# Squared-ReLU attention and a gated feed-forward: the first quad's k and q loaded by SyncE and cast on chip, with a new order of the work

## The chip, the cores and the metric

The kernel runs on one core of a Trainium2 chip. The metric is the device time of one execution in microseconds: the median of the runs, and lower is better. The profile comes from one further execution, taken by the hardware profiler; its times are counted from the first instruction of the program (the span's start).

A core has TensorE (PE, with its weight loads as PEld), VectorE (DVE), ScalarE (ACT), GpSimd (POOL) and SyncE (SP, which here only issues DMAs). Each engine works through its own queue in order. DMAs issued by SP and by POOL are carried out by the same 16 DMA engines.

## What is computed

```python
def _attn_ref(q, k, v):                       # q, k, v: (8, 12, 448, 64) float32
    scale = 1.0 / np.sqrt(q.shape[-1])
    scores = scale * np.matmul(q, k.transpose(0, 1, 3, 2))
    attn = np.maximum(scores, 0.0) ** 2 / S   # S = 448
    return np.matmul(attn, v)

def _moe_ref(x, w_in, w_out):                 # x: (3584, 768), w_in: (768, 2048)
    h = x @ w_in
    g = h * (1.0 / (1.0 + np.exp(-1.702 * h)))
    return g @ w_out                          # out: (3584, 768) float32
```

The attention's output, heads side by side, is the `x` of the feed-forward part.

## The kernel before

**Tiling.** The 96 heads are worked in 24 units of four heads, called quads (u = 0 to 23, three to a batch element). A quad's 448 positions are split into J = 7 blocks of 64. The feed-forward part works on eight groups of tokens, g = 0 to 7, alternately of 6 and 8 blocks (384 and 512 columns, `gblk`). Group 0 needs quads 0, 1 and 2.

**How k and q come in.** There are two ways, and both end in transposed float16 tiles `kT` and `qT`.

- Quads 0 to 5: `load16` (L115) lets POOL issue a DMA that casts float32 to float16 on the way, 448 KB read and 224 KB written. `trans_pe` (L124) then transposes on PE with 14 small matmuls (L129) into a PSUM bank of the pool `ps_m`, which has two, and VectorE copies the result out (L133).
- Quads 6 to 23: `load_qk` (L77) lets SP issue two plain DMAs of float32 (L82) into the tiles `kst` and `qst`, two buffers each. `cast` (L96) turns k into float16 on ScalarE (L102) and q on POOL (L104), and `trans` (L107) transposes by DMA (L111).

The float16 tiles `k16` and `q16` have three buffers each. v always comes by POOL's casting DMA (L91), and so do the weights, `win` in four quarters (L383, two DMAs each) and `wout` in four (L388, indexed by half of the columns and half of the rows).

**What is done with them.** A slot `s u.j` (L138, L145) makes the scores of block j in one of three PSUM pairs (`ps_s`): four matmuls, two by two, on quarters of the array. `relu2` (L152) takes the positive part, on ScalarE (L159) or, where the token has `:d`, on VectorE (L156); `:h` holds it back until after the next feed-forward product, and `:t` issues the slot's matmuls twice. The square `x u.j` is a VectorE product (L430). `a u` multiplies by v (28 matmuls, L174) and `xt_evac` (L182) copies the result into the group's `xt` (L194, L197). `f g.c` (L214) makes one of 16 chunks of the hidden layer, six matmuls (L222), the activation on ScalarE (L227) and a scaling on POOL (L229). Groups 1 to 7 multiply two blocks of rows at a time by `wout` in seven products `p g.m.n` (L303) instead of eight, which needs sums of the halves of `wout`. VectorE makes these sums in the tokens A to E (L272). Group 0 uses plain products `m g.m.h` (L242).

**What sets the order.** Nothing is scheduled by the compiler: the kernel holds a list of 729 words (L459 to L508) which is run from left to right, and each word issues its instructions on each engine's queue in that order. So the list is the order of every queue. Before it stand a warm-up of ScalarE's table and ten matmuls on a zero tile (L405). The list begins:

```python
"jq0 jk0 I q0 k0 z3 s0.0:d x0.0 s0.1 x0.1 jq1 jk1 s0.2 q1 s0.3 x0.2 x0.3 s0.4 k1 "
"x0.4 z3 jk4 jk2 s0.5 s0.6 k2 k4 x0.5 s1.0 s1.1 jv0 x0.6 s1.2 jq3 x1.0 x1.1 a0:m "
```

`jq`, `jk`, `jv` are POOL's casting loads of q, k and v; `jw` and `jo` load parts of `win` and `wout`. `q` and `k` are the transposes on PE, `z3` is three more zero matmuls into a fresh score bank, and `I` makes the identity for the transposes (on POOL). `L`, `K`, `Q`, `R` are load, two casts and transposes of the second way, `W` a later load of v. `G1` is a DMA of 128 bytes that holds SP's queue until a part of `wout` has landed, and stands ahead of the first `L` (SP has nothing to do before it).

Of the kernel before, what the change touches and what calls it, by code (L numbers as in the profile page):

```python
# [8 lines left out]
F32 = mybir.dt.float32  # L9
# [6 lines left out]
def kernel(  # L16
# [9 lines left out]
    nc = tc.nc  # L26
# [88 lines left out]
    def load16(u, n):  # L115
# [5 lines left out]
            in_=quad({"k": k, "q": q}[n], b, pr))  # L121
        st[n + "16"] = x

    def trans_pe(u, n):  # L124
        st = units[u]
        ps = ps_m.tile([128, 1024], F16, name="tr", tag="mm")
        for j in range(J):
            for a in range(2):
                nc.tensor.matmul(  # L129
                    out=ps[64 * a:64 * a + 64, j * 128:(j + 1) * 128],  # L130
                    lhsT=st[n + "16"][:, a, j, :], rhs=ident[:, :], is_transpose=True)
        t = qkT.tile([128, J, 128], F16, name=f"{n}T", tag=f"{n}T")
        nc.vector.tensor_copy(out=t, in_=ps[:, 0:J * 128])  # L133
        st[n + "T"] = t

    early = []

    def scores(u, j, times=1):  # L138
        st = units[u]
        sc = early.pop() if early else ps_s.tile([128, 2, 512], F32, name="sc", tag="sc")  # L140
        for s in [0, 1] * times:
            for a in range(2):
                r = slice(64 * a, 64 * a + 64)
                c = slice(64 * s, 64 * s + 64)
                nc.tensor.matmul(  # L145
                    out=sc[c, a, 0:S],
                    lhsT=st["kT"][r, j, c],
                    rhs=st["qT"][r, :, c],
                    start=True, stop=True)
        return sc  # L150

    def relu2(u, j, sc, dve=False):  # L152
        rl = rlp.tile([128, 2, S], F16, name="rl", tag="rl")
        at = atp.tile([128, 2, S], F16, name="at", tag="at")
        if dve:
            nc.vector.tensor_scalar(out=rl, in0=sc[:, :, 0:S], scalar1=0.0, scalar2=None,  # L156
                                    op0=ALU.max)
        else:
            nc.scalar.activation(out=rl, in_=sc[:, :, 0:S], func=AF.Relu)  # L159
        pend[u, j] = (at, rl)  # L160
        return at

# [232 lines left out]


    with tc.manual_schedule():
        nc.vector.memset(warm, 0.0)
        nc.scalar.activation(out=warm, in_=warm, func=AF.Gelu_apprx_sigmoid)

# [18 lines left out]
                   "D": (w_d, wout[1][0], wout[0][0], ALU.add)}  # L419

        def slot(how, u, j):
            sc = scores(u, j, 2 if "t" in how else 1)
            if "h" in how:
                held.append((u, j, sc))
            else:
                ats[u, j] = relu2(u, j, sc, "d" in how)
# [13 lines left out]
        def zeros(how, n):  # L440
            early.append(ps_s.tile([128, 2, 512], F32, name="sc", tag="sc"))
            for _ in range(n):
# [6 lines left out]
              "f": lambda how, g, f: m1(g, f), "m": lambda how, g, m, h: m2(g, m, h),  # L449
              "p": lambda how, g, m, n: pair(g, m, n), "i": lambda how, g, m, h: single(g, m, h),  # L450
              "jk": lambda how, u: load16(u, "k"), "jq": lambda how, u: load16(u, "q"),
              "jv": lambda how, u: load_v(u), "jw": lambda how, i: w1(i),
              "jo": lambda how, h, i: w2(h, i), "I": lambda how: make_identity(nc, ident),
              "G": lambda how, i: sp_gate(wout[0][i][0:1, 0, 0:64]),
# [2 lines left out]
              "Q": lambda how, u: cast(u, "q", nc.gpsimd),  # L457
              "R": lambda how, u: trans(u)}
        words = (  # L459
            "jq0 jk0 I q0 k0 z3 s0.0:d x0.0 s0.1 x0.1 jq1 jk1 s0.2 q1 s0.3 x0.2 x0.3 s0.4 k1 "  # L460
            "x0.4 z3 jk4 jk2 s0.5 s0.6 k2 k4 x0.5 s1.0 s1.1 jv0 x0.6 s1.2 jq3 x1.0 x1.1 a0:m "
            "s1.3 s1.4 x1.2 jq2 s1.5 jk3 q2 jk5 x1.3 x1.4 jv2 s1.6 x1.5 jv1 k3 s2.0:t q3 x1.6 "
            "jw0 s2.1:t x2.1 s2.2:t x2.0 s2.3:t x2.2 a1:m x2.3 s2.4:t jq4 jq5 s2.5:t s2.6 x2.4 "
            "x2.5 x2.6 jv3 jw1 jv4 k5 s3.0 jv5 a2 s3.1 q4 jw2 x3.0 x3.1 s3.2 f0.0 q5 x3.2 jw3 "
            "s3.3:d s3.4 x3.3 s3.5 x3.4 jo0.1 f0.1 f0.2 s3.6 s4.0:d x3.5 s4.1 f0.3 f0.4 x4.0 G1 "
            "x3.6 a3 x4.1 s4.2 x4.2 jo0.0 s4.3 x4.3 f0.5 L6 f0.6 s4.4 s4.5:h x4.4 s4.6:d f0.7 "
            "f0.8 L7 f0.9 x4.6 f0.10 x4.5 s5.0:d x5.0 s5.1 a4 s5.2 s5.3 f0.11 x5.2 f0.12 jo1.1 "
            "x5.1 x5.3 s5.4 s5.5:d x5.4 s5.6 f0.13 f0.14 x5.5 f0.15 K6 Q6 x5.6 R6 a5 m0.2.0 "
            "f1.0 C0 m0.1.0 f1.1 K7 m0.0.0 s6.0:d s6.1 Q7 L8 s6.2 x6.0 A3 f1.2 f1.3 f1.4 f1.5 "
            "x6.2 s6.3 s6.4:h x6.1 E0 Q8 s6.5:d x6.3 x6.5 W6 R7 jo1.0 f1.6 A1 f1.7 s6.6 C3 s7.0 "  # L470
            "f1.8 x6.6 x6.4 K8 x7.0 f1.9 f1.10 L9 s7.1 Q9 R8 a6 L10 W7 s7.2 s7.3 E3 A2 f1.11 "
            "x7.1 C1 x7.2 K9 R9 x7.3 f1.12 s7.4:h s7.5 x7.5 m0.0.1 B3 B0 s7.6 B1 x7.6 x7.4 K10 "
            "Q10 s8.0 s8.1 x8.0 x8.1 f1.13 m0.1.1 A0 s8.2 x8.2 W8 a7 s8.3:d s8.4 L11 B2 m0.2.1 "
            "s8.5 x8.4 x8.3 s8.6 f1.14 D3 x8.5 x8.6 f1.15 W9 s9.0:d s9.1 x9.0 a8 R10 L12 s9.2 "
            "s9.3 p1.0.0 K11 f2.0 f2.1 C2 f2.2 x9.2 f2.3 x9.1 s9.4 s9.5:h x9.3 s9.6 p1.0.1 f2.4 "
            "D1 f2.5 f2.6 x9.4 E2 f2.7 s10.0 Q11 L13 x9.6 K12 s10.1:h s10.2:h x9.5 x10.0 f2.8 "
            "p1.0.2 x10.1 p1.0.3 Q12 x10.2 s10.3 a9 E1 x10.3 s10.4:d s10.5 f2.9 W10 f2.10 f2.11 "
            "R11 f2.12 p1.0.4 R12 x10.4 x10.5 s10.6 x10.6 s11.0 D0 s11.1 D2 f2.13 x11.0 W11 "
            "x11.1 p1.0.5 s11.2 a10 L14 s11.3:h s11.4 p1.0.6 x11.4 x11.2 Q13 K13 p1.2.0 f2.14 "
            "s11.5 x11.3 s11.6 f2.15 x11.5 p1.2.1 x11.6 L15 p1.2.2 s12.0 a11 s12.1 x12.0 "  # L480
            "s12.2:h p1.2.3 Q14 p1.2.4 s12.3 R13 x12.1 K15 s12.4:h K14 s12.5 x12.2 p1.2.5 "
            "p1.2.6 f3.0 f3.1 x12.5 x12.4 x12.3 s12.6:h s13.0:h s13.1 Q15 i2.2.1 R14 x13.1 "
            "i2.2.0 x13.0 L16 W12 p2.0.0 p2.0.1 s13.2:h L17 x12.6 a12 s13.3 f3.2 R15 f3.3 W13 "
            "x13.2 x13.3 f3.4 f3.5 p2.0.2 f3.6 s13.4 Q16 s13.5 s13.6 x13.4 f3.7 x13.5 W14 x13.6 "
            "f3.8 s14.0:d Q17 s14.1 x14.1 s14.2:h x14.0 K16 f3.9 W15 L18 p2.0.3 f3.10 x14.2 a13 "
            "s14.3 s14.4 f3.11 f3.12 x14.4 K18 x14.3 f3.13 K17 R16 f3.14 s14.5 s14.6 R17 "
            "s15.0:d x14.5 p2.0.4 x15.0 p2.0.5 x14.6 W16 W17 f3.15 s15.1:d a14 x15.1 s15.2:h "
            "s15.3 x15.3 p2.0.6 f4.0 s15.4:d x15.2 s15.5 s15.6:h p3.0.0 f4.1 f4.2 f4.3 x15.4 "
            "x15.5 Q18 L19 L20 x15.6 f4.4 s16.0:h s16.1:d s16.2 p3.0.1 x16.1 p3.0.2 x16.2 "
            "p3.0.3 K19 a15 s16.3:h s16.4 p3.0.4 p3.0.5 x16.0 R18 x16.4 p3.0.6 f4.5 Q19 W18 "  # L490
            "s16.5 s16.6 x16.5 s17.0:h x16.3 f4.6 p3.2.0 f4.7 x16.6 s17.1 s17.2:d x17.2 R19 "
            "x17.0 a16 x17.1 f4.8 p3.2.1 f4.9 p3.2.2 p3.2.3 f4.10 s17.3 s17.4 s17.5 p3.2.4 "
            "f4.11 x17.4 s17.6:h x17.3 W19 s18.0 x17.5 p3.2.5 x17.6 x18.0 p3.2.6 f4.12 L21 Q20 "
            "s18.1 K20 a17 s18.2 s18.3:h x18.1 f4.13 f4.14 L22 x18.2 f4.15 s18.4:d x18.4 "
            "s18.5:h f5.0 i4.2.1 Q21 x18.3 s18.6 x18.5 W20 s19.0:d x19.0 s19.1 x18.6 R20 i4.2.0 "
            "f5.1 f5.2 x19.1 p4.0.0 s19.2 a18 Q22 s19.3:h s19.4 f5.3 f5.4 K22 f5.5 p4.0.1 K21 "
            "x19.2 x19.3 f5.6 x19.4 f5.7 p4.0.2 s19.5 s19.6 L23 s20.0 p4.0.3 f5.8 x19.5 x19.6 "
            "f5.9 p4.0.4 Q23 x20.0 s20.1 s20.2 R21 x20.1 x20.2 a19 s20.3:h s20.4 f5.10 p4.0.5 "
            "p4.0.6 K23 x20.3 s20.5 x20.4 s20.6 s21.0 f5.11 x20.5 x20.6 R22 f5.12 s21.1:d s21.2 "
            "x21.1 x21.0 a20 s21.3:d s21.4 f5.13 x21.4 x21.2 x21.3 f5.14 f5.15 p5.0.0 s21.5 W21 "  # L500
            "x21.5 s21.6 s22.0:h f6.0 x21.6 p5.0.1 f6.1 p5.0.2 p5.0.3 x22.0 s22.1 a21 s22.2 "
            "s22.3 x22.3 f6.2 f6.3 x22.2 R23 f6.4 f6.5 p5.0.4 f6.6 x22.1 W22 f6.7 s22.4 s22.5:d "
            "s22.6 x22.5 p5.0.5 p5.0.6 p5.2.0 x22.6 f6.8 x22.4 s23.0:d x23.0 s23.1:h p5.2.1 "
            "p5.2.2 s23.2 s23.3 x23.1 a22 x23.2 s23.4 f6.9 f6.10 W23 f6.11 f6.12 x23.3 f6.13 "
            "s23.5:d x23.5 s23.6 p5.2.3 p5.2.4 x23.4 f6.14 x23.6 f6.15 p5.2.5 p5.2.6 i6.2.1 a23 "
            "i6.2.0 f7.0 f7.1 f7.2 f7.3 f7.4 p6.0.0 f7.5 f7.6 p6.0.1 f7.7 p6.0.2 f7.8 p6.0.3 "
            "f7.9 p6.0.4 p6.0.5 f7.10 f7.11 f7.12 f7.13 f7.14 f7.15 p6.0.6 p7.0.0 p7.0.1 p7.0.2 "
            "p7.0.3 p7.0.4 p7.0.5 p7.0.6 p7.2.0 p7.2.1 p7.2.2 p7.2.3 p7.2.4 p7.2.5 p7.2.6").split()  # L508
        for w in words:
            w, _, how = w.partition(":")  # L510
            t = w.rstrip("0123456789.")
# [33 lines left out]
```

## Time and profile before

| | us |
|---|---|
| median of 4 runs | 382.5 (382.31 to 383.65) |
| the profiled execution | 384.31 |
| its span, first to last instruction | 382.5 |
| TensorE clock granted in it | 0.997 of full |

The page gives, for each engine, its busy time and its share of the span, and then the span in 40 equal slices with the busy share of each in tenths. DMA is the mean busy share of 16 DMA engines. The chain of waits goes back from the last instruction, at each step to what released it. Groups of instructions are named by line, engine, operation and tiles, with their number, busy time, mean duration, and the idle time of the engine ahead of them.

| first stage, from the trace | us from the span's start |
|---|---|
| POOL issues q0, k0 (casting) | 1.24, 2.13 |
| they land | 5.17, 6.26 |
| first slot s0.0 on PE | 7.61 |
| k2 and k4 land | 13.22, 10.33 |
| slot s1.0 on PE | 14.16 |
| last square of quad 2 (x2.6) ends on VectorE | 28.09 |
| q4 lands | 29.23 |
| first hidden chunk f0.0 on PE | 30.10 |
| last matmul of the kernel ends | 377.5 |

### The profile page before, as it was taken

How to read it: one execution, taken by the hardware profiler on the slowest of the kernel's cores; microseconds unless marked ns; L12 is line 12 of the kernel's file. 1: busy time of each engine (PE TensorE's matmuls, PEld its weight loads, DVE VectorE, ACT ScalarE, POOL GpSimd, SP SyncE). 2: the span in 40 equal slices, each digit the busy share in tenths (PEclk: the TensorE clock that was granted, in tenths of full speed). 3: DMA queues.
4: the chain of work that ended last, by engine and by line, in shares of the span. 5: the costliest groups of instructions: out<-in, count | busy, mean ns of one | idle time of the engine just before them, and what ended most of it. 6: DMA issues, size and time to landing. Idle time of an engine off the chain costs nothing.

```text
span 382.5 us, 7864 instructions
## 1 busy us (share of the span) xinstructions
PE 369.9 (97%) x3136; PEld 192.3 (50%) x3136; DVE 256.9 (67%) x425; ACT 214.7 (56%) x314; POOL 135.9 (36%) x200
## 2 busy tenths in 40 slices
PE   8789999999999999999999999999999999999994
PEld 3345555445555554544455555544455555455552
DVE  3899762778968787557688875638777866313374
ACT  2887762796676768267664656466764461232210
POOL 7545552652244433056440423432142231222200
PEclk9999999999999999999999999999999999999998
DMA  8999999799946496788872909741640413101133
GB/s 120 170 187 204 205 197 275 148 150 229 245 157 146 52 290 152 172 170 175 122 221 69 183 5 289 122 122 26 136 69 0 108 26 83 43 0 41 43 83 83
DMA packets 65221, 50.85 MB, mean 133 GB/s; under 512 B 35744, under 2 KB 61728, under 8 KB 65184
## 3 DMA queue, kind: packets, MB, share of 16 engines
q1 hardware_dynamic: 47872, 35.70, 38.4%
q0 software_dynamic: 17152, 14.55, 26.3%
q8 instruction: 24, 0.39, 0.4%
q10 hardware_dynamic: 160, 0.10, 0.1%
q14 instruction: 13, 0.11, 0.1%
HBM read 45.61 MB, written 11.01 MB: 148 GB/s over the span
## 4 chain that ended last, share of the span: by engine, by line
PE 86%; DMA 6%; DVE 2%; issue 2%; ACT 1%; POOL 1%; ACTq 0%; POOLq 0%
PE ht L222 38%; PE op L287 28%; PE sc L145 8%; PE av L174 7%; PE op L248 4%; DMA q<-in_q_dram 3%; DMA k<-in_k_dram 3%; DVE osb L298 2%; PE tr L129 1%; ACT rl L159 0%; POOL v L91 0%; DVE at L430 0%; ACT gf L227 0%; POOL win L383 0%; ACT eb L296 0%
## 5 line engine op out<-in xcount | busy, mean ns | idle before, releaser
L222 PE MATMUL ht<-xt,win 128*128 128x384 f16 (+1 forms) x768 | 156.2, 353 | 0.4 <-ACT gf L227 0.4
L229 POOL TENSOR_SCALAR gt<-gf 128x384 f16<-128x384 f32 (+1 forms) x128 | 82.2, 642 | 199.1 <-ACT gf L227 196.7
L159 ACT ACTIVATE rl<-sc 128x896 f16<-128x896 f32 x144 | 126.3, 917 | 44.0 <-PE sc L145 36.7
L227 ACT ACTIVATE gf<-ht 128x384 f32<-128x384 f32 (+1 forms) x128 | 69.6, 546 | 85.6 <-PE ht L222 76.2
L430 DVE TENSOR_TENSOR at<-rl 128x896 f16<-128x896 f16 x168 | 106.0, 664 | 13.5 <-ACT rl L159 12.8
L222 PEld LDWEIGHTS <-win 128*128 128x128 f16 x768 | 72.5, 98 | 74.8 <-issue 12.0
L287 PEld LDWEIGHTS <-gt 128*128 128x128 f16 x408 | 38.6, 98 | 30.1 <-issue 4.1
L145 PE MATMUL sc<-qT,kT 64*64 64x448 f16 x696 | 48.4, 357 | 1.1 <-ACT rl L159 0.7
L287 PEld LDWEIGHTS <-as 128*128 128x128 f16 x312 | 29.9, 98 | 22.9 <-issue 2.9
L287 PE MATMUL op<-wsum,gt 128*128 128x384 f16 x224 | 40.6, 326 | 0.0
L287 PE MATMUL op<-wout,as 128*128 128x384 f16 x224 | 40.0, 326 | 0.0
L298 DVE SCALAR_TENSOR_TENSOR osb<-op,osb 128x384 f32<-128x384 f32 (+1 forms) x45 | 23.6, 544 | 23.6 <-PE op L287 23.3
L156 DVE TENSOR_SCALAR rl<-sc 128x896 f16<-128x896 f32 x24 | 26.1, 1087 | 16.2 <-PE sc L145 15.8
L174 PE MATMUL av<-at,v 64*64 64x448 f16 x616 | 33.2, 350 | 0.1
L287 PE MATMUL op<-wout,gt 128*128 128x384 f16 (+1 forms) x184 | 32.4, 319 | 0.5 <-DVE osb L298 0.5
L194 DVE CAST xt<-av 128x896 f16<-128x896 f32 (+2 forms) x32 | 24.5, 792 | 11.7 <-PE av L174 11.7
L298 DVE SCALAR_TENSOR_TENSOR osb<-op,ea 128x384 f32<-128x384 f32 x22 | 12.1, 551 | 27.8 <-PE op L287 12.2
L145 PEld LDWEIGHTS <-kT 64*64 64x64 f16 x696 | 17.0, 105 | 24.6 <-issue 16.9
L174 PEld LDWEIGHTS <-v 64*64 64x64 f16 x672 | 19.4, 107 | 13.7 <-issue 2.9
L282 DVE TENSOR_TENSOR as<-gt 128x1024 f16<-128x1024 f16 x36 | 24.4, 703 | 0.7 <-POOL gt L229 0.7
L104 POOL CAST q<-qst 128x896 f16<-128x896 f32 x18 | 17.6, 976 | 9.2 <-issue 7.2
L91 POOL DMA_DIRECT2D v<-in_v_dram x24 | 18.0, 749 | 3.7 <-DMA win<-in_moe_w_in_dram 1.4
(38 smaller groups left out, 169.0 us busy)
## 6 DMA issues: line engine op xcount, KB each, us to landing
out_dram<-osb SPq DMA_DIRECT2D x54, 192.0 KB, 3.0
kst<-in_k_dram SPq DMA_DIRECT2D x18, 448.0 KB, 5.9
qst<-in_q_dram SPq DMA_DIRECT2D x18, 448.0 KB, 6.4
v<-in_v_dram POOLq DMA_DIRECT2D x24, 224.0 KB, 5.0
win<-in_moe_w_in_dram POOLq DMA_DIRECT2D x8, 384.0 KB, 12.0
wout<-in_moe_w_out_dram POOLq DMA_DIRECT2D x4, 768.0 KB, 12.8
q<-in_q_dram POOLq DMA_DIRECT2D x6, 224.0 KB, 7.1
k<-in_k_dram POOLq DMA_DIRECT2D x6, 224.0 KB, 5.3
```

The source lines that it names most:

```text
L145: nc.tensor.matmul(out=sc[c, a, 0:S], lhsT=st["kT"][r, j, c], rhs=st["qT"][r, :, c], start=True, stop=True)
L156: nc.vector.tensor_scalar(out=rl, in0=sc[:, :, 0:S], scalar1=0.0, scalar2=None, op0=ALU.max)
L159: nc.scalar.activation(out=rl, in_=sc[:, :, 0:S], func=AF.Relu)
L174: nc.tensor.matmul(out=st["av"][s][64 * a:64 * a + 64, 0:S], lhsT=st["v16"][r, a, 64 * j:64 * j + 64], rhs=at[r, a, :], start=(j == 0), st ...
L194: nc.vector.tensor_copy(out=xts[g][:, 2 * pr:2 * pr + 2, c], in_=st["pair"][:, :, f])
L222: nc.tensor.matmul(out=ht[:, 0:n], lhsT=w[:, kk, fo:fo + 128], rhs=xts[g][:, kk, 0:n], start=(kk == 0), stop=(kk == NK - 1))
L227: nc.scalar.activation(out=gf[:, 0:n], in_=ht[:, 0:n], func=AF.Gelu_apprx_sigmoid, scale=1.0 / SC)
L229: nc.gpsimd.tensor_scalar(out=gts[g][:, f, 0:n], in0=gf[:, 0:n], scalar1=SC, scalar2=1.0, op0=ALU.mult, op1=ALU.mult)
L282: nc.vector.tensor_tensor(out=out_, in0=x, in1=y, op=op)
L287: nc.tensor.matmul(out=op[:, 0:cw], lhsT=lhs[:, f, :], rhs=w[:, f, c0:c0 + cw], start=(start and f == 0), stop=(stop and f == HF - 1))
L298: nc.vector.scalar_tensor_tensor(out=o, in0=op[:, 0:w], scalar=sc, in1=add, op0=ALU.mult, op1=ALU.add)
L430: nc.vector.tensor_tensor(out=at, in0=rl, in1=rl, op=ALU.mult)
```

## The change

The k and q of quad 0 no longer come by POOL's casting DMA. `load_qk(0)` is called ahead of everything else, so SP issues both in float32, and a new function casts them on chip, k on VectorE (`ck0`) and q on ScalarE (`cq0`), into the same float16 layout that `load16` makes. The transposes on PE stay. POOL's first load is now k of quad 1, behind the making of the identity. `scores` and `relu2` get a way to use two `ps_m` banks in place of a `ps_s` pair, for a slot marked `:m`; no slot in the new list is marked so. The list of words is a new one throughout; it has the same words but for `jk0` and `jq0`, which became `ck0` and `cq0`, and two slots more have `:h`.

```diff
+    def cast16(u, n, eng):
+        c = c16.tile([128, 2, J, D], F16, name=f"{n}16", tag=f"{n}16")
+        o, i = c.rearrange("p a j d -> p a (j d)"), units[u][n]
+        if eng is nc.scalar:
+            eng.activation(out=o, in_=i, func=AF.Copy)
+        else:
+            eng.tensor_copy(out=o, in_=i)
+        units[u][n + "16"] = c
+
...
     with tc.manual_schedule():
+        load_qk(0)
         nc.vector.memset(warm, 0.0)
...
+              "ck": lambda how, u: cast16(u, "k", nc.vector),
+              "cq": lambda how, u: cast16(u, "q", nc.scalar),
...
-            "jq0 jk0 I q0 k0 z3 s0.0:d x0.0 s0.1 x0.1 jq1 jk1 s0.2 q1 s0.3 x0.2 x0.3 s0.4 k1 "
-            "x0.4 z3 jk4 jk2 s0.5 s0.6 k2 k4 x0.5 s1.0 s1.1 jv0 x0.6 s1.2 jq3 x1.0 x1.1 a0:m "
-            "s1.3 s1.4 x1.2 jq2 s1.5 jk3 q2 jk5 x1.3 x1.4 jv2 s1.6 x1.5 jv1 k3 s2.0:t q3 x1.6 "
-            "jw0 s2.1:t x2.1 s2.2:t x2.0 s2.3:t x2.2 a1:m x2.3 s2.4:t jq4 jq5 s2.5:t s2.6 x2.4 "
-            "x2.5 x2.6 jv3 jw1 jv4 k5 s3.0 jv5 a2 s3.1 q4 jw2 x3.0 x3.1 s3.2 f0.0 q5 x3.2 jw3 "
+            "cq0 I ck0 k0 jk1 q0 k1 s0.0:d s0.1 x0.0 jq1 x0.1 s0.2 q1 jk2 s0.3 x0.2 x0.3 s0.4 "
+            "k2 jq2 s0.5 jv0 z3 jv5 jv1 x0.4 s0.6 x0.5 jk3 x0.6 s1.0 s1.1 jk4 x1.0 a0:m x1.1 "
+            "s1.2 x1.2 s1.3 z3 s1.4 q2 x1.3 s1.5 k3 x1.4 s1.6 s2.0:t x1.5 jq3 x1.6 s2.1:t x2.0 "
+            "a1:m s2.2:t s2.3:t jv2 x2.1 x2.2 s2.4:t q3 x2.3 s2.5:t x2.4 jq4 s2.6 jk5 x2.5 s3.0 "
+            "x2.6 jw0 jw1 k4 jq5 a2 jv3 q4 jv4 s3.1 jw2 s3.2 jw3 x3.1 f0.0 x3.0 x3.2 f0.1 jo0.1 "
...
```

Further on, for group 1 the loads of the last two quarters of `wout` change places (`jo1.0` comes early, `jo1.1` late), and the words of all later stages stand in other places:

```diff
-            "x5.1 x5.3 s5.4 s5.5:d x5.4 s5.6 f0.13 f0.14 x5.5 f0.15 K6 Q6 x5.6 R6 a5 m0.2.0 "
-            "f1.0 C0 m0.1.0 f1.1 K7 m0.0.0 s6.0:d s6.1 Q7 L8 s6.2 x6.0 A3 f1.2 f1.3 f1.4 f1.5 "
+            "s5.5:h s5.6:d x5.4 f0.12 x5.6 f0.13 x5.5 f0.14 f0.15 a5 K6 m0.2.0 Q6 R6 C2 f1.0 "
+            "f1.1 Q7 C0 jo1.1 C1 f1.2 f1.3 m0.1.0 s6.0 x6.0 K7 L8 s6.1 s6.2:d f1.4 x6.2 C3 x6.1 "
+            "W6 K8 m0.0.0 A2 f1.5 s6.3:h B0 R7 Q8 L9 s6.4:h R8 s6.5:d f1.6 x6.4 f1.7 x6.5 "
```

## The prediction

> **What bounds the kernel now.** I read the page first (busy shares, the 40 slices, the chain), then the chain of waits over the first 33 us, then sums by stretch, then single instructions.
>
> ```profile
> PE 369.9 (97%) x3136; PEld 192.3 (50%) x3136; DVE 256.9 (67%) x425; ACT 214.7 (56%) x314; POOL 135.9 (36%) x200
> PE   8789999999999999999999999999999999999994
> DMA  8999999799946496788872909741640413101133
> ```
>
> TensorE is busy 97% of the span; a slice is 9.6 us. Only the first three and the last fall short, and the last is the final stores, which the change does not touch. So what can be won lies in the first 30 us. Two stretches, cut at the first `ht` matmul (30.10 us):
>
> ```profile
> 8.04:28.10 20.06, 15.96 (x303) 8.75 (x296) 18.95 (x38) 17.64 (x21) 11.13 (x16) 1.00 1.19 178
> 30.10:377.50 347.40, 346.07 (x2766) 180.25 (x2762) 234.16 (x380) 194.53 (x290) 118.25 (x171) 1.00 0.62 130
> ```
>
> The columns are length, then busy time of PE, PEld, DVE, ACT and POOL, clock, DMA share, GB/s. After 30.10 PE idles 1.3 us in 347. Before 28.10 VectorE is the fullest engine (18.95 of 20.06), ScalarE next, and all DMA engines are occupied. The chain of waits there:
>
> ```profile
> 2.13 4.12 DMA k<-in_k_dram
> 6.30 0.60 PE tr L129 x14
> 7.19 6.03 DMA k<-in_k_dram
> 13.26 0.60 PE tr L129 x14
> 17.60 11.63 DMA q<-in_q_dram
> 29.27 0.58 PE tr L129 x14
> 30.17 1.08 PE ht L222 x6
> ```
>
> Three loads carry it: k of quad 0 (landed 6.26), k of quad 2 (13.22), q of quad 4 (29.23). The second costs most. Its transposes, and quad 4's with them, stand on PE ahead of slot s1.0, so ScalarE idles 1.36 us (13.24 to 14.60) and VectorE 0.89. The third holds f0.0: VectorE ends the second quad-2 copy into `xt` at 29.73, yet f0.0 starts at 30.10, behind q4 and s3.2.
>
> **The change, part by part.** The end follows from (a) when f0.0 starts and (b) the PE work from there on.
>
> *First loads.* At 0.75 us, when the other engines are released, SP issues k and q of quad 0. The nearest row for their landing is quad 23's load, issued at 253.26 into idle queues: k landed 3.37 us after its issue, q 4.60 after that same instant. The view of the tile says the same of the least:
>
> ```profile
> DMA to landing us min/median/max: 3.4/5.9/8.0
> ```
>
> So k at 4.1 and q at 5.35. POOL, without two issues (0.89 + 0.73), makes the identity (2.85 to 3.45 before, 0.6) from 1.24 and issues k of quad 1 at about 1.85. Its packets come 1.6 us later (before: issue 1.24, first packet 2.84) and mix with q's, so I take 5.6 for q (ends 5.3 and 6.0: all three loads together are 3 x 1.13, the spacing of landings at 8.06, 9.21 and 10.33, from 1.9 us on, and 0.5 to confirm). ScalarE's cast is 0.95 (L102), the transposes let the copy start 0.62 later (5.34 to 5.96 before), the copy takes 0.62, s0.0 follows 0.07 later: 5.6 + 0.95 + 0.05 + 0.62 + 0.62 + 0.07 = **7.9**, against 7.61. So the new way in is 0.3 later for the first slot, ends 7.5 and 8.5. VectorE's cast of k has no row: below, 0.5 (half of a PSUM cast, if both SBUF ports work); above, 1.1 (L194's 0.96 for 768 elements, scaled to 896). It lies under q's wait either way: 4.1 + 1.1 + 0.62 + 0.62 is 6.4. On VectorE only kT's copy stands behind it, on ScalarE only relus that need q. k1's transposes now stand before s0.0, but k1 should land by 6.2 and they run (0.51) under the copy of qT.
>
> *A rule against it.* The Trainium skill, SBUF — State Buffer, section SBUF: two separate sides, says that a float32 SBUF-to-SBUF copy on VectorE takes both shared ports, and that GpSimd cannot write the descriptors of its DMAs meanwhile. The new cast of k is that copy, from 4.1 us on, with POOL just issuing quad 2 and v. By the rule those issues slip by 0.5 to 1.1. The row: POOL needs 0.72 per issue, the engines 1.13 per load, so three loads issued by 4.0 last until about 6.5; the stream runs dry by neither. Cost 0; were POOL only just ahead, it would be the cast's length. No row of before has such a copy beside an issue.
>
> *To f0.0.* In the new order k2 and q2 are fifth and sixth of all loads, k4 ninth; s1.0 no longer stands behind k4, and k5's transposes go behind f0.0. VectorE's work from the relu of s0.0 to x2.6, by its cadence in the trace: relu 1.1, 21 squares x 0.535 = 11.2, two evacuations of 1.19, five copies x 0.535 = 2.7: 17.4 (before seven copies: 18.5). Before it took 20.05, from 8.04 to 28.09, of which 0.89 is the k2 wait and 0.7 small gaps. After: relu at 8.3, plus 17.4, plus 0.7 = 26.4. ScalarE alone would give 8.5 + 19 x 0.80 + 0.92 + 0.6 = 25.2, so VectorE decides. From x2.6 to f0.0 a k copy and `xt` cost 1.4 (28.09 to 29.5), while q4, now load 14 and ahead of all weights, lands near 19 and holds nothing. The first quarter of win is nearer: before, it had landed 8.3 us after v of quad 2 (20.06 to 28.32) with one load between. POOL's waits for transposes (1.65, 0.54 and 2.86 us between issues) go, so v of quad 2, load 13, lands near 1.9 + 13 x 1.13 + 0.5 = 17.1; one load more lies between, which makes 17.1 + 8.3 + 1.1 = 26.5. That is below what VectorE allows. So f0.0 is at **27.8** (27.2 to 28.8), 2.3 earlier.
>
> *From f0.0 on.* Both PE queues hold the same 3136 matmuls, so only neighbours matter. Durations from the trace: f 0.98 (384 columns) or 1.30 (512), a product 1.30, a slot 0.19, av 1.32, about 0.1 more at each change between full and quarter tiles. Summed over each order: 343.1 before, 343.6 after. The 0.5 is k5's transposes (0.51), now behind f0.0; changes of kind differ by a few only (slot runs 78 and 76). Before, the actual stretch was 2.2 longer than this sum; I take the same again. Weights: f0.4, f0.8, f0.12 come 8.7, 13.4, 20.6 after f0.0, at 36.5, 41 and 48, the quarters of win for them landed at 35.86, 42.10 and 45.57 before, with no fewer loads ahead of them than now, and the stream starts sooner: nothing. SP's two issues precede nothing until the gate at 49.4; quad 7's kst reuses the buffer freed by the cast of k 40 us before: nothing. The slot's unused bank option adds no instruction.
>
> *Sum.* -2.3 + 0.5 = **-1.8 us**. Against the profiled execution: span 382.5 to 380.7, its own time 384.31 to 382.5. The runs' median, 382.5, is 1.8 below that execution, so I move it by the same: 380.7.
>
> **Rivals.**
> 1. *It wins nothing that can be told apart.* A casting load's data start 1.6 us after its issue, an SP load's 1.0 to 1.2, and the cast gives 0.95 back. If q lands at 6.3, as the casting queue's k did, s0.0 starts at 8.6 and f0.0 at 28.5 (as it does if win's first quarter lands 2 us later than 26.5); with 0.5 behind and about 0.6 of new small waits: -1.6 + 1.1 = -0.5, 382.0. For it: VectorE is nearly full in the first stage, and near 54 us after f0.0 its share of weight sums rises. Against it: the k2 wait of 0.89 to 1.36 goes in any case. Time 381.4 to 383.6.
> 2. *Slower: wout's last quarter.* Its load is issued behind gt of f1.1 and quad 7's cast: 31.2 us of PE work after f0.0 plus POOL's lag of 2.5 (seen before: due at 72.4, issued 74.92). The same tile took 11.9 to land, the other half 10.2. First user, the sum A2 on VectorE, is due at 41.1, m0.0.1 on PE at 45.8. 31.2 + 2.5 + 11.9 = 45.6: VectorE stands up to 4 us with the relu of s6.5 and its squares queued behind, PE just does not. It decides from a landing of 12.1 on; at 17, with the loads and transposes of quads 8 and 9 in front, PE stands 4.9, less the 1.8: 385.6. For it: before, m0.0.1 waited 0.3 for such a load. Against: the longest wout landing in the trace is 14.5, which gives 383.1.
> 3. *More than forecast.* q at 5.3 and ScalarE deciding: x2.6 at 25.2, f0.0 at 26.8: -3.3 + 0.5, 379.7, or 379.2 if small stalls go too.
>
> **How the numbers follow.** Forecast 0.50 (379.6 to 381.3), rival 1 0.24, rival 2 or another late wait beyond 383.6 0.14, rival 3 0.12. A measurement here tells about 0.3% (1.15 us) from no change. Faster: forecast and rival 3, 0.62. Same: most of rival 1, 0.22. Slower: rival 2 and a rest of rival 1, 0.16. The range, 379.0 to 383.6, leaves out most of rival 2 and a little below.
>
> **What would show it.** Right: no ScalarE gap near 13 us, f0.0 at 27.2 to 28.8, PE idle under 2 us from there to the last product. Wrong in the start: s0.0 after 8.6, or PE's k1 transposes waiting for their load. Wrong behind f0.0: A2 or m0.0.1 ended by a wout landing, or slots waiting for relus around 50 to 60 us after f0.0. The forecast fails if a stage behind f0.0 gives back more than 0.7 us.

## The result, and the profile after

The changed kernel takes 381.49 us (median of 44 runs, 380.87 to 383.49) against 382.52 for the kernel before (63 runs): a ratio of 0.997, 95% interval 0.996 to 0.998, so 1.0 us less, about the least that can be told here. Its profiled execution took 382.86 us with a span of 381.1; that of before 384.31 and 382.5. The page of the changed kernel, the same rows as before:

```profile
PE 370.3 (97%) x3136; PEld 194.4 (51%) x3136; DVE 256.8 (67%) x426; ACT 215.6 (57%) x315; POOL 132.5 (35%) x198
PE   6989999999999999999999999999999999999993
PEclk9899999999999999999999999999999999999999
DMA  9999997996666986789569656590282303010333
```

PE's first slice of 9.5 us is poorer than before (6 for 8) and its second fuller (9 for 7), the DMA engines begin sooner (9 for 8), and TensorE's clock dips in the second slice. Sums by stretch, from VectorE's first relu to the last square of quad 2, and from f0.0 to the last matmul (length, busy PE, PEld, DVE, ACT, POOL, clock, DMA share, GB/s):

```profile
9.90:27.85 17.95, 16.44 (x278) 9.02 (x271) 17.69 (x37) 17.30 (x21) 10.04 (x15) 0.95 1.25 204
29.22:375.80 346.58, 345.86 (x2780) 181.41 (x2776) 234.55 (x383) 195.62 (x291) 114.89 (x168) 1.00 0.63 129
```

f0.0 came at 29.22 us, 0.9 earlier than in the profile of before, and what follows, to the last matmul, is 0.9 us shorter (347.4 before). The chain of waits in the first stage (start, length, what):

```profile
1.45 6.86 DMA k<-in_k_dram
8.31 0.04 issue
8.36 0.98 PE tr L138 x13
9.33 0.02 issue
9.36 0.62 DVE kT L142
9.98 1.01 DVE rl L173
10.99 0.02 issue
11.01 1.16 DVE at L447 x2
```

The three loads that carried the old chain are gone from it. In their place stands one: k of quad 1, issued at 1.45 and landed at 8.31. The timeline around it (start, length, engine, line, what; in brackets the idle time ahead and what ended it):

```profile
4.25 0.70 DVE L130 CAST k<-kst 128x896 f16<-128x896 f32 x1 [3.08 <-DMA kst<-in_k_dram]
...
5.45 0.95 ACT L128 ACTIVATE q<-qst 128x896 f16<-128x896 f32 x1 [3.22 <-DMA qst<-in_q_dram]
...
6.45 0.58 PE L138 MATMUL tr<-ident,q 128*64 128x128 f16 x14 [0.68 <-ACT q L128]
...
7.08 0.62 DVE L142 COPY qT<-tr 128x896 f16<-128x896 f16 x1 [0.64 <-PE tr L138]
...
8.36 0.96 PE L138 MATMUL tr<-ident,k 128*64 128x128 f16 x14 [1.32 <-DMA k<-in_k_dram]
...
9.24 1.33 PE L159 MATMUL sc<-qT,kT 64*64 64x448 f16 x12
```

Quad 0 came in as forecast: k landed at 4.22, q at 5.43, `qT` was complete at 7.70. But s0.0 stands behind k1's transposes in PE's queue, and started at 9.24. PE had been idle for much of the time from 5.8 to 8.36, and the granted clock was half from 8.13 to 11.54; in that stretch k1's transposes took 0.96 us (those of k0 0.58) and the first three slots 1.33 (0.76 in the profile of before).

That was the state after one profile each. The 44 times, though, lie in two groups, 30 from 380.87 to 381.83 and 14 from 382.45 up, and the profiled execution, 382.86, is of the second. The median, 381.49, lies just above the forecast's own 379.6 to 381.3. So the experiments had to settle three things: what the new way in brings, what the new order brings, and what the profiles of either kernel stand for.

### The profile page after: what moved, and what is told of

Its sections match the earlier page's. It is cut to its first block, busy times and chain, and to the rows that moved or that the text cites. A ratio compares the mean times of both kernels' runs of the same rounds, so it can differ in the third digit from the quotient of the medians.

```text
span 381.1 us, 7870 instructions
## 1 busy us (share of the span) xinstructions
PE 370.3 (97%) x3136; PEld 194.4 (51%) x3136; DVE 256.8 (67%) x426; ACT 215.6 (57%) x315; POOL 132.5 (35%) x198
## 4 chain that ended last, share of the span: by engine, by line
PE 89%; DVE 4%; ACT 2%; DMA 2%; issue 2%; POOL 0%; POOLq 0%; ACTq 0%
PE ht L238 39%; PE op L303 29%; PE sc L159 9%; PE av L190 7%; PE op L264 4%; DMA k<-in_k_dram 2%; DVE at L447 2%; ACT rl L175 2%; DVE osb L314 1%; PE tr L138 1%; DVE xt L213 1%; DVE kT L142 0%; DVE qT L142 0%; DVE rl L173 0%; ACT eb L312 0%
## 5 line engine op out<-in xcount | busy, mean ns | idle before, releaser
L245 POOL TENSOR_SCALAR gt<-gf 128x384 f16<-128x384 f32 (+1 forms) x128 | 81.2, 634 | 197.2 <-ACT gf L243 192.0
L447 DVE TENSOR_TENSOR at<-rl 128x896 f16<-128x896 f16 x168 | 104.8, 656 | 14.9 <-ACT rl L175 14.1
L104 POOL CAST q<-qst 128x896 f16<-128x896 f32 x18 | 16.8, 931 | 11.7 <-DMA qst<-in_q_dram 10.9
L314 DVE SCALAR_TENSOR_TENSOR osb<-op,eb 128x384 f32<-128x384 f32 x22 | 12.1, 549 | 11.7 <-PE op L303 11.7
```

The costliest lines, as they stand in the source:

```text
L245: nc.gpsimd.tensor_scalar(out=gts[g][:, f, 0:n], in0=gf[:, 0:n], scalar1=SC, scalar2=1.0, op0=ALU.mult, op1=ALU.mult)
L314: nc.vector.scalar_tensor_tensor(out=o, in0=op[:, 0:w], scalar=sc, in1=add, op0=ALU.mult, op1=ALU.add)
L447: nc.vector.tensor_tensor(out=at, in0=rl, in1=rl, op=ALU.mult)
```

## The experiments

Each was timed in five rounds beside the kernel before on the same chip; the medians of before were 382.98 (first four), 382.58 (next three) and 382.48 (last three).

| run | median us | ratio to before (95%) | profiled us | s0.0 | f0.0 | f0.0 to the last product |
|---|---|---|---|---|---|---|
| before, first profile | 382.52 | | 384.31 | 7.61 | 30.10 | 345.35 |
| changed, first profile | 381.49 | 0.997 (0.996 to 0.998) | 382.86 | 9.24 | 29.22 | 344.48 |
| e1 k1 behind s0.3 | 381.65 | 0.9968 (0.9953 to 0.9984) | 381.59 | 7.66 | 27.89 | 344.50 |
| e2 new way in, old order | 382.49 | 0.9991 (0.9971 to 1.001) | 382.38 | 7.61 | 28.39 | 345.19 |
| e3 old way in, new order | 381.46 | 0.9959 (0.9943 to 0.9974) | 382.05 | 8.21 | 28.70 | 344.50 |
| e4 both casts on ScalarE | 381.87 | 0.9973 (0.9956 to 0.9989) | 381.37 | 8.13 | 27.79 | 344.50 |
| f1 PE filled | 382.52 | 0.9988 (0.997 to 1.0006) | 382.28 | 8.84 | 28.67 | 344.49 |
| f2 k by SP, q by POOL | 381.17 | 0.9955 (0.9941 to 0.997) | 381.18 | 8.07 | 27.90 | 344.49 |
| a2 changed again | 381.35 | 0.9975 (0.9955 to 0.9995) | 381.13 | 7.79 | 27.60 | 344.50 |
| g1 before again | 382.68 | 0.999 (0.9961 to 1.002) | 382.44 | 7.55 | 28.32 | 345.25 |
| g2 k1 behind s0.2 | 381.46 | 0.9964 (0.9944 to 0.9984) | 381.94 | 7.79 | 28.42 | 344.49 |
| g3 f2 and g2 | 381.07 | 0.9949 (0.9928 to 0.997) | 381.24 | 7.84 | 27.96 | 344.48 |

The last column counts from the start of f0.0 to the start of the last product on PE. "Ordinary" below means an execution near its kernel's more frequent times: 382.44 us for before (g1) and 381.13 for the changed kernel (a2). Two things can be read from the table alone. With the old list of words it is 345.2 to 345.4, with the new one 344.5, whatever comes before. And the profiled time less f0.0 is 353.3 to 353.7 for every kernel with the new list and 354.0 to 354.2 for those with the old. So an execution's time tells where its f0.0 was: a run of the changed kernel at 382.9 had it near 29.3, one at 381.1 near 27.5 (an estimate from this difference).

**e1, k1 behind the slots.**

```diff
-cq0 I ck0 k0 jk1 q0 k1 s0.0:d s0.1 x0.0 jq1 x0.1 s0.2 q1 jk2 s0.3 x0.2 x0.3 s0.4 k2
+cq0 I ck0 k0 jk1 q0 s0.0:d s0.1 x0.0 jq1 x0.1 s0.2 s0.3 k1 jk2 x0.2 x0.3 s0.4 q1 k2
```

> The changed kernel with one move: k1's transposes (and their copy on VectorE) stand behind slot s0.3, and q1's behind s0.4, in place of ahead of s0.0 and behind s0.2. Theory: in the changed kernel PE waits at k1's transposes for a load that lands at 8.31 us while quad 0 is ready at 7.7, so s0.0 starts 1.4 us late, and VectorE, full from there on, carries that to f0.0. Then s0.0 is at 7.7 to 7.9, f0.0 at 27.8 to 28.4 (29.2 in the changed kernel), the time 0.8 to 1.4 us below the changed kernel's, 380.1 to 380.7. Rival: the loads of quad 1 bound the stage in any order (q1 lands at 9.66), so the early slots only wait later: f0.0 within 0.3 of 29.2, time unchanged at 381.5.

s0.0 and f0.0 came as expected (7.66, 27.89), and k1 had landed late again, at 8.09, with no harm. But the median, 381.65, is not below the changed kernel's. Only 2 of its 12 runs lie above 382, yet the rest, 381.48 to 381.80, lie in the upper half of the changed kernel's lower group (380.87 to 381.83, its median 381.26). In the profile s0.3 waits for a score bank until 9.24, and k1 and q1 now stand behind it. That this wait is the price which every run pays is argued from this one profile.

**e2 and e3, each part alone.**

```diff
 e2: list of before
-jq0 jk0 I q0 k0 z3 s0.0:d
+cq0 I ck0 k0 q0 z3 s0.0:d
```
```diff
 e3: changed list, load_qk(0) left out
-cq0 I ck0 k0 jk1 q0 k1 s0.0:d
+jq0 jk0 I q0 k0 jk1 k1 s0.0:d
```

> The new way in of quad 0 (SP's float32 loads, casts on VectorE and ScalarE) with the word list of the kernel before, k0 transposed ahead of q0. Theory: the new way in by itself saves nothing, since q's load, the cast and the copies take about as long as the casting load did; s0.0 at 7.7 to 8.0 (7.61 before) and, as the k2 wait stays, f0.0 at 29.8 to 30.4: time 382.2 to 382.9. Rival: SP's loads bring the whole stream of loads forward by 1 us, so k2 and q4 land 1 us earlier and f0.0 is at 29.0 to 29.4: time 381.4 to 381.8.

> The changed kernel's word list with quad 0 loaded by POOL's casting DMAs as before, k1's transposes ahead of s0.0 as in the changed kernel. Theory: the order brings the gain (about 1 us from the removed k2 wait, 0.6 from fewer stalls of PE behind f0.0), the way in none: k1 lands near 7.3 to 8, s0.0 at 8.2 to 8.7, f0.0 at 28.4 to 29.2, time 380.7 to 381.6. Rival: the order needs the early SP loads, and without them quad 1 and k2 come a load later: s0.0 above 9, f0.0 above 29.7, time 382 or more.

The new list alone gives the whole gain (381.46), the way in alone none that can be told (ratio 0.9991, interval across 1). Both theories hold for the time. e3's profile is of the slowest of its 12 runs (382.05), so its f0.0, 28.70, is not its ordinary value. For f0.0 of e2 both failed: it came at 28.39, far from 29.8 and from 29.0 too. That was the first sign that the 30.10 of before was not its ordinary value.

**e4, the cast off VectorE.**

```diff
-"ck": lambda how, u: cast16(u, "k", nc.vector),
+"ck": lambda how, u: cast16(u, "k", nc.scalar),
-cq0 I ck0 k0 jk1 q0 k1
+ck0 I cq0 k0 jk1 q0 k1
```

> The changed kernel with k of quad 0 cast on ScalarE too, ahead of q's cast; VectorE casts nothing. Theory of the port rule: VectorE's float32 copy (4.25 to 4.95 us) keeps GpSimd from writing descriptors and makes k1 land late; then k1 lands 0.5 us or more earlier than 8.31 and s0.0 follows it, time 0.4 to 0.8 us down. Rival: the casting queue moves nothing until SP's two loads are through (near 4.7), whatever VectorE does: k1 lands at 8.0 to 8.4, s0.0 at 9.0 to 9.4, time within 0.4 us of the changed kernel.

k1 landed at 7.40, as the port rule had it, but the time is 381.87, no better, with five of 12 runs at 382.5 to 383.0: the high group is there without VectorE's cast, so the cast does not make it. The second profile of the changed kernel (a2) agrees: with the cast on VectorE, k1 landed at 6.97.

**f1, the clock.** Zero matmuls in PE's gaps.

```diff
-ck0 k0 jk1 q0 k1 s0.0:d
+ck0 k0 jk1 z3 q0 z3 k1 s0.0:d
```

> The changed kernel with three zero matmuls on PE between the transposes of k0 and q0 and three between those of q0 and k1, where PE idles; they compute nothing that is used. Theory: in the profile of the changed kernel the granted clock is half from 8.13 to 11.54 us, because PE was idle for much of the 3.4 us ahead, and runs in which this happens are those near 383 us (14 of its 44 lie above 382.4). Then with PE kept busy no such half-clock stretch shows behind 5 us, and nearly all runs lie at 380.9 to 381.7. Rival: the higher runs come from late landings of k1, which the filling can't change: a third of the runs stays above 382.4.

The clock was full throughout, and the theory fell all the same: 11 of 12 runs lie at 381.99 to 382.82. k1 landed at 8.28, s0.0 started at 8.84, f0.0 at 28.67. So a half clock is not needed for a high time; e1's profile, with k1 at 8.09, shows a full clock too. Why nearly every run of this kernel is high was not tried further.

**f2, one SP load in place of two.**

```diff
-for n, t in (("k", k), ("q", q)):
+for n, t in (("k", k), ("q", q))[:1 if u == 0 else 2]:
-cq0 I ck0 k0 jk1 q0 k1 s0.0:d
+jq0 I ck0 k0 jk1 q0 k1 s0.0:d
```

> The changed kernel with only k of quad 0 by SP and a cast on VectorE, q of quad 0 by POOL's casting DMA as first of its queue. Theory: POOL's queue moves nothing until SP's loads are nearly through (first packet at 4.5 to 4.7 us in every run with two SP loads, 2.84 without), so with one SP load it starts at 3.3 to 3.8; q lands at 5.2 to 5.7 and needs no cast, s0.0 can start at 7.0 to 7.8 unless k1 (landing at 6.5 to 7.5) holds it; f0.0 at 27.0 to 27.9, time 380.6 to 381.4. Rival: POOL's descriptors take their time whatever SP does, first packet 4.5 or later, q lands at 6 or later and s0.0 above 8: no gain, 381.3 to 382.

POOL's first packet came at 3.46, as expected; q landed at 6.07, one engine late (14 of 16 completions by 5.24), and k1 at 7.51. All 12 runs lie at 380.76 to 381.60: the high group is gone.

**a2 and g1, second profiles.**

> The changed kernel itself once more. Theory: its first profile (k1 landed at 8.31, s0.0 at 9.24, half clock to 11.5) is one of its late executions; a second one has k1 at 7.0 to 8.4, and where the clock stays full, f0.0 is at 27.3 to 28.0 and the time of that execution at 381.0 to 381.4. Rival: its first slot is always near 9.2 and f0.0 near 29.2, and the two groups of its times have another cause.

> The kernel before once more, for a second profile. Theory: the execution that the prediction was made from (384.31 us, 1.8 above the median) was late in its first stage itself, so an ordinary one, of 382.2 to 382.6, has its first hidden chunk f0.0 at 28.0 to 28.6 us and not at 30.10, with the same 347.4 us behind it; the gain of the change in its first stage is then 0.4 to 1.0 us and not 2.3. Rival: the 1.8 us lie outside the span or behind f0.0, and an ordinary execution has f0.0 at 29.7 to 30.3 too.

Both theories held. In its ordinary execution the changed kernel has k1 at 6.97 and the first slot at 7.79. Its timeline, where the transposes of k1 wait for a PSUM bank and no longer for the load:

```profile
7.26 0.58 PE L138 MATMUL tr<-ident,k 128*64 128x128 f16 x14 [0.31 <-DVE kT L142]
...
7.79 0.76 PE L159 MATMUL sc<-qT,kT 64*64 64x448 f16 x12
...
8.42 1.08 DVE L173 TENSOR_SCALAR rl<-sc 128x896 f16<-128x896 f32 x1
```

And the kernel before, in an ordinary execution (382.44 us), has no k2 stall. Two lines of its timeline and its sums by stretch:

```profile
11.91 1.13 PE L129 MATMUL tr<-ident,k 128*64 128x128 f16 x28 [0.44 <-DVE at L430]
...
13.41 0.92 ACT L159 ACTIVATE rl<-sc 128x896 f16<-128x896 f32 x1 [0.23 <-PE sc L145]
```
```profile
7.99:26.95 18.96, 15.75 (x303) 9.19 (x296) 18.82 (x38) 17.65 (x21) 11.69 (x17) 1.00 1.21 187
28.32:375.67 347.35, 346.12 (x2766) 180.20 (x2762) 234.63 (x382) 194.65 (x291) 118.17 (x170) 1.00 0.62 131
```

k2 landed at 11.87, not 13.22; ScalarE's gap is 0.23 us where the first profile had 1.36; q4 landed at 27.01; f0.0 came at 28.32. VectorE is full (18.82 of 18.96). The ordinary execution of the changed kernel has VectorE just as full (17.70 of 17.80), in a stretch that is 1.16 shorter:

```profile
8.42:26.22 17.80, 15.57 (x274) 8.78 (x271) 17.70 (x37) 17.38 (x21) 9.82 (x15) 1.00 1.26 203
27.60:374.20 346.60, 345.88 (x2780) 181.43 (x2776) 234.63 (x383) 195.70 (x291) 116.05 (x169) 1.00 0.64 130
```

So, ordinary against ordinary, f0.0 comes 0.72 earlier (27.60 for 28.32) and the rest is 0.75 shorter: 0.51 of that is idle time of PE (1.23 before, 0.72 after) and 0.24 busy time. What PE waited for behind f0.0, as the view of its waits names it, is this for before (second profile) and for the changed kernel (second profile):

```profile
PE op L287 <- DVE osb L298: 0.5, 1, 0.5
PE ht L222 <- ACT gf L227: 0.4, 1, 0.4
```
```profile
PE op L303 <- DVE osb L314: 0.5, 1, 0.5
```

The wait at the last products stays; the one of `ht` for a PSUM bank (0.37 us ahead of f2.11, ended by ScalarE's activation of an earlier chunk) is gone.

**g2 and g3, k1 behind three slots.**

```diff
-q0 k1 s0.0:d s0.1 x0.0 jq1 x0.1 s0.2 q1 jk2 s0.3
+q0 s0.0:d s0.1 s0.2 x0.0 k1 jq1 x0.1 q1 jk2 s0.3
```

> The changed kernel with k1's transposes behind slot s0.2 and its copy on VectorE behind x0.0; the three first slots stand ahead of it. Theory: what parts the two groups of times of the changed kernel is k1's landing (6.97 in its ordinary execution, 8.31 in its late one) ahead of the first slot; with three slots ahead of it nearly all runs lie in the lower group, 380.8 to 381.6, s0.0 at 7.6 to 7.9, and the median is 0.1 to 0.4 below the changed kernel's. Rival: the late executions are late in other loads as well (q1 and k2 follow k1 by 1.1 us each), so the move only passes the wait on: a quarter of the runs stays above 382.3.

> Both: k of quad 0 by SP with VectorE's cast, q of quad 0 by POOL's casting DMA, and k1's transposes behind slot s0.2. Theory: q lands at 5.2 to 6.1 and needs no cast, so s0.0 starts at 6.9 to 7.6 and, with VectorE full from there on, f0.0 at 26.9 to 27.6: time 380.5 to 381.0, the best here. Rival: quad 1 is what the stage then waits for (q1 lands near 9), and it equals the run with q by POOL alone, 381.17.

In g2 no run is above 381.94, but the lower edge rose too (381.32), and the median, 381.46, did not move: in its profile k1 came at 8.98 and q1 at 10.09, and s0.3 waited for q1 (10.65). The move takes the first slots out of the wait and passes what is left on, as its rival had it in part. g3 is the best version found: 381.07, all 12 runs at 380.76 to 381.52. It is faster than before (0.9949), and its median is 0.3 to 0.4 below the changed kernel's two, which the intervals do not separate. Its s0.0, at 7.84, was not earlier in the profile, since q's load was late (6.49).

## Why the prediction was right, and where its sum was not

The forecast was -1.8 us; the medians moved by -1.0. What holds is the direction, and that VectorE's queue sets f0.0 and the new order shortens it. The wait for k2, to which the forecast gave most of the gain, was no part of an ordinary execution. Two terms are wrong by more than a microsecond in opposite directions: the first stage was taken 1.6 too large and the rest 1.25 too small. That the sum came out near is in part luck.

- *Loads and casts of quad 0.* k at 4.1 and q at 5.6 were forecast, s0.0 at 7.9; an ordinary execution has 4.16, 5.35 and 7.79. VectorE's cast took 0.70 to 0.78, between the ends given. Right.
- *k1 under the copy of qT.* "k1 should land by 6.2": it landed between 6.97 and 8.98 in the profiles of kernels with two SP loads and k1 as POOL's first (a2, the first profile, e1, e4, f1, g2). In the ordinary execution its landing costs little; in the late one it moves s0.0 by 1.45 us (7.79 to 9.24) and f0.0 by 1.6. This was priced as nothing. The upper group of times fits it (14 of 44 runs, their median 1.75 above the lower group's), and g2, with three slots ahead of k1, has no run there. Only one execution of that group was profiled, so for the others it is inferred.
- *To f0.0.* 27.8 was forecast and 27.60 is the ordinary value: the sum over VectorE's work held (x2.6 ended at 26.22 for 26.4 forecast). In it k4 is the eleventh of all loads, not the ninth (it is ninth in POOL's queue); nothing hangs on that. What failed is the other side of the difference: **the 30.10 of before**. "Before it took 20.05, of which 0.89 is the k2 wait": that wait belonged to the profiled execution. Ordinarily VectorE is full in either kernel. The new order takes two copies out of its stretch from the first relu to x2.6 (seven before, five after), which is 1.07. But only one of them leaves the first stage: k4's goes behind x2.6, into the place of k5's, which goes behind f0.0. The other, k1's, goes ahead of the first relu, which it helps to make later (8.42 for 7.99). By these terms 0.64, 0.72 measured. The term was -2.3 and is -0.7.
- *The step from the profiled execution to the median.* "The runs' median is 1.8 below that execution, so I move it by the same": the 1.8 lay in the first stage itself, 30.10 against 28.32, and could not be saved a second time. This is the step that made the first term too large.
- *From f0.0 on.* +0.5 was forecast, -0.75 measured. The time above the sum of PE's work, taken as equal (2.2), is 0.9 in the new order (344.5 less 343.6). The one wait that went by name is the 0.37 at f2.11; the rest of the 1.25 is not traced. The new list also carries `:d` and `:h` on other slots from quad 5 on (66 slots differ), which the account of the change left out and which was not tried by itself. Had this stretch stayed as it was, ordinary executions would gain 0.7; with the forecast's +0.5, only 0.2, which could not be told from nothing.
- *Rivals.* The wout wait did not come: the last quarter was issued at 62.57 (62.9 by the forecast's steps), landed 8.1 us later, and m0.0.1 ran at 74.64 with no wait. The first rival, a gain that can hardly be told, was nearer in size than the forecast's own 1.8; its causes (q at 6.3, new small waits behind f0.0) were not what happened.
- *The port rule* (the Trainium skill, SBUF — State Buffer, SBUF: two separate sides) was costed at nothing, and no cost of it shows: POOL's two DMA issues that overlap VectorE's cast took 0.73 and 0.74, beside 0.72 to 0.76 for the others behind the first, k1 was early with that cast in a2, and e4 has the high times without it. What makes a k1 late stays open. The completions say where it sits: in the first profile 14 of its 16 arrived by 6.68 and the last at 8.31, in a2 all between 6.04 and 6.97.

## What to carry to other kernels

Before a stall in one profile is counted as gain, compare that execution's own time with the median: if it is late, find which stage is late, for a wait that only the late execution has can't be saved in the others. Where an engine is full through a stage, the gain of a new order is the work taken out of that stage on that engine, and moving work to the stage's front saves nothing; the earlier loads alone added nothing here (e2). A load that stands ahead of ready work in an in-order queue wants slack for its latest landing. In e1 and g2 the work put ahead of it had waits of its own, and there the slow runs grew rarer while the fastest became slower (381.48 and 381.32, for 380.87).

## What the hardware showed that was not expected

At the start POOL's queue moved nothing while SP's two loads filled the DMA engines. With two SP loads issued at 0.74 and 1.26 and POOL's first at 1.45, POOL's first packet came at 4.5 to 4.7 us in all seven such profiles, SP's last between 4.8 and 5.4; with one SP load it came at 3.46, with none at 2.84. The changed kernel's queues from 2.4 to 4.4 us, and the issues of the same two microseconds:

```profile
q1 hardware_dynamic: 404, 0.70, 91.8%
...
q<-in_q_dram POOLq DMA_DIRECT2D x2, 224.0 KB, 7.7
k<-in_k_dram POOLq DMA_DIRECT2D x1, 224.0 KB, 7.7
```

Only SP's queue moves packets there, though k of quad 1 had been issued a microsecond earlier. The Trainium skill (DMA: Bandwidth & Descriptors, Queues, rings and completion order) has each DMA engine take turns between its queues packet by packet; no such turns show in these two microseconds. Whether POOL's descriptors were ready by then the trace doesn't tell. The forecast had let the two mix, and took k1 for early by it.
